# Rows chosen by a scatter through DRAM instead of a matmul, in a sigmoid-attention and mixture-of-depths kernel

## The chip, the cores and the metric

The kernel runs on one core of one Trainium2 chip. The metric is the device time of one execution in microseconds (us). Before the change three runs gave 446.25, 447.38 and 449.26 us; the median is 447.38.

## The reference, cut to what matters

Sigmoid attention for 8 sequences (12 heads, 448 tokens, head dimension 64), all in float32; its output, laid out as 8 x 448 x 768, goes into a mixture-of-depths block. There each token has a score (its row times `w_gate`), and in each sequence the 128 tokens of the highest scores go through a two-layer network and are added back, weighted by the sigmoid of the score.

```python
scores = scale * np.matmul(q, k.transpose(0, 1, 3, 2)) - np.log(S)
attn_out = np.matmul(1.0 / (1.0 + np.exp(-scores)), v)      # (8, 12, 448, 64)
x = attn_out.transpose(0, 2, 1, 3).reshape(8, 448, 768)
scores = np.einsum('bsd,d->bs', x, w_gate)
out = x.copy()
for b in range(8):
    top_idx = np.argpartition(-scores[b], 128)[:128]
    xe = x[b, top_idx]
    ye = np.maximum(xe @ w1, 0.0) @ w2                        # 768 -> 1024 -> 768
    g = 1.0 / (1.0 + np.exp(-scores[b, top_idx]))
    out[b, top_idx] = xe + g[:, None] * ye
```

## The kernel before, in words

**Steps and slots.** The 8 x 12 heads are 24 groups of four heads, three to a sequence. A step `s` (0 to 11) treats two groups, and has seven slots `n` (0 to 6), each for two of the fourteen 32-token pieces of each group. A slot issues 32 score matmuls (`score`, L339: k times q, into the two-bank PSUM tiles `PA[0]` and `PA[1]`), two sigmoids on ScalarE (`squash`, L353) and 32 value matmuls (`value`, L368, accumulating into the four PSUM banks `PO[x][pr]`, where `x` is the group of the step). The value matmuls run four slots behind the scores, so those of step `s - 1` end with slot 3 of step `s`. Then the accumulated outputs leave PSUM: `takes(s - 1, x)` are two transposes on VectorE (L389) for each `x`, into the sequence's rows `x_b`, which SyncE stores to `out` (L406).

**The order.** The schedule is manual: every engine, and every DMA queue, executes in the order in which the program issues; semaphores come from the tracked reads and writes of tiles. The function `after(s, n)` holds what follows slot `n`: loads, transposes of q and k on VectorE (L313, L321), gates, rankings, weight sums (`make_sum`, L208) and stores.

**Blocks.** In the steps named in `BLOCKS`, slot 3 is followed by a block of the mixture-of-depths network: `block(s)` (L680) runs the takes and a list of items. An item ("c", b) is the choice of sequence b's rows, ("t", b) turns the chosen rows (`turn_rows`, six transposes on TensorE at L524, copied by ScalarE), and (1, p, key) or (2, p, key) is one of the seven products of the first or the second layer of a pair of sequences p (a seven-product scheme with sums of weight quarters; L560 and L624, 12 or 4 matmuls in the program, each recorded twice). `places` gives each item its PSUM bank in turn. In steps whose successor has a block, and in the range `LATE` (from the first block's step on), the value matmuls are issued in another order (`first_slots`, `last_slot`, `rounds`, `split`): in `last_slot` the values of `x = 0` end before those of `x = 1`; in a `split` slot those of `x = 0` end last.

**From scores to rows.** When a sequence's rows are complete, `gate(b)` forms its scores on VectorE and GpSimd writes them to DRAM (L425); `spread(b)` reads them back into all 128 partitions (`rep`, L437, GpSimd's queue). `ranking(b)`, issued in the slot `RANKED[b]` (sequence 1: in step `FIRST`), counts for each token how many have a higher score or the same score and a lower number: eight passes over `rep` on VectorE (L445, L448). `place` adds the counts and compares them with the 128 places, a one-hot matrix (`hot`, L460). For sequences 2 to 5 VectorE multiplies the one-hot by row number and score and sums over four columns (L469, L473). `choose` (L482, L486) finishes with matmuls: row number and score by place, in PSUM. `fetch` copies them to SBUF (L493, L496) and gathers the rows from `out` with an indirect DMA on GpSimd's queue (L506); the result goes back to `out` with an indirect scatter on the same queue (L644). The last two sequences are treated in `rest`, after step 11.

**Values.** `load_v(s)` (L133) brings the values of a step: on SyncE's queue up to step 4, on ScalarE's from step 5 on.

## Time and profile before

| | us |
|---|---|
| runs, median (lowest to highest) | 447.38 (446.25 to 449.26) |
| profiled execution, its own time | 446.79 |
| its span | 445.0 |
| TensorE matmuls busy | 430.2 |
| VectorE busy | 302.6 |
| ScalarE busy | 191.2 |
| GpSimd busy | 32.8 |
| matmuls of the choices (L482, L486), all eight sequences | 6.4 |
| sums on VectorE for the choices (L469, L473) | 10.7 |
| one-hot on VectorE (L460), eight times | 5.5 |
| eight passes of all rankings (L445, L448) | 43.4 |

A line of the instruction views has start, duration, engine, source line, operation, output and inputs, their shapes, a count, and in brackets the idle time of the engine before it with what ended that. PE is TensorE's matmul, PEld its weight load, DVE VectorE, ACT ScalarE, POOL GpSimd, SP SyncE. A line of windows has the stretch, its length, the busy time of the five engines (with counts), the granted TensorE clock, the DMA engines' share and their GB/s.

### The profile page before, as it was taken

The page shows a single profiled execution, that of the slowest core. Times are in us where ns is not written, and L with a number is a line of the kernel's source. Part 1 is how long each engine was busy: PE and PEld are TensorE (multiplying, and loading weights), DVE is VectorE, ACT ScalarE, POOL GpSimd, SP SyncE. Part 2 cuts the span into 40 slices and gives each one's busy share as a digit, 9 for nine tenths or more (in the row PEclk, how much of TensorE's full clock was granted, in tenths as well). Part 3 has the DMA queues.
Part 4 walks back from the last instruction along what each step waited for, and adds up shares of the span by engine and source line. Part 5 has one row for each costly group of instructions (what it writes and reads, how often), then busy time and mean ns, then how long its engine had stood idle before and what let it go on. Part 6 is the DMA issues. An engine that isn't in the chain of part 4 may idle for free.

```text
span 445.0 us, 14349 instructions
## 1 busy us (share of the span) xinstructions
PE 430.2 (97%) x6374; PEld 259.2 (58%) x6374; DVE 302.6 (68%) x639; ACT 191.2 (43%) x257; POOL 32.8 (7%) x55
## 2 busy tenths in 40 slices
PE   7999999999999999999999999999999999999994
PEld 3456554444457568455447559546545749769952
DVE  4316368964958986966997885835796669883462
ACT  4666666666654633641660670552363330101100
POOL 7000000000001000100002000010000101001001
PEclk9999999999999999999999999999999999999998
DMA  8984835999645997699656598499945964611001
GB/s 234 246 249 110 300 87 114 212 186 232 200 143 120 233 308 186 181 234 298 219 181 177 154 234 147 138 224 241 269 167 107 190 219 63 119 36 72 1 0 71
DMA packets 112846, 76.80 MB, mean 173 GB/s; under 512 B 90304, under 2 KB 99136, under 8 KB 112784
## 3 DMA queue, kind: packets, MB, share of 16 engines
q1 hardware_dynamic: 106768, 61.55, 53.7%
q0 software_dynamic: 1984, 7.91, 6.2%
q10 hardware_dynamic: 4032, 6.42, 6.1%
q8 instruction: 50, 0.82, 0.8%
q14 instruction: 12, 0.10, 0.1%
HBM read 55.41 MB, written 20.46 MB: 170 GB/s over the span
## 4 chain that ended last, share of the span: by engine, by line
PE 88%; DVE 5%; ACT 3%; issue 1%; DMA 1%; POOLq 0%; ACTq 0%; DVEq 0%
PE a L339 27%; PE o L368 25%; PE o L624 12%; PE o L560 10%; PE a L560 7%; PE a L624 4%; ACT attn L353 2%; PE p L989 1%; DVE spare L208 1%; PE p L339 1%; DMA out_dram<-xe,idx 1%; ACT hidden L353 1%; DVE scr L448 1%; DVE scr L445 1%; DVE scr L397 1%
## 5 line engine op out<-in xcount | busy, mean ns | idle before, releaser
L339 PE MATMUL a<-qT,kT 32*64 32x448 f32 x2624 | 242.4, 537 | 0.6 <-DVE got L496 0.5
L353 ACT ACTIVATE attn<-a,bias_s 128x896 f32<-128x896 f32 x162 | 161.4, 1007 | 83.8 <-PE a L339 79.8
L368 PE MATMUL o<-attn,raw_v 32*64 32x448 f32 x2176 | 194.6, 536 | 0.5 <-issue 0.4
L339 PEld LDWEIGHTS a<-qT,kT 32*64 32x64 f32 x2624 | 92.8, 131 | 87.1 <-ACT attn L353 49.2
L368 PEld LDWEIGHTS o<-attn,raw_v 32*64 32x64 f32 x2176 | 74.3, 131 | 35.0 <-issue 26.9
L389 DVE STREAM_TRANSPOSE x_b<-o 128x448 f32<-128x448 f32 x48 | 27.8, 623 | 46.7 <-PE o L368 26.8
L368 PE MATMUL o<-attn,rows_t 32*64 32x448 f32 x448 | 42.3, 537 | 0.2 <-issue 0.2
L576 ACT ACTIVATE hidden<-hidden 128x512 f32<-128x512 f32 x12 | 7.5, 630 | 68.5 <-DVE hidden L573 68.5
L400 DVE TENSOR_REDUCE gate_p<-scr 128x14 f32<-128x448 f32 x48 | 29.8, 622 | 1.7
L321 DVE STREAM_TRANSPOSE kT<-raw_k 128x448 f32<-128x448 f32 x42 | 24.1, 613 | 8.8 <-DMA raw_k<-in_k_dram 7.6
L397 DVE TENSOR_TENSOR scr<-x_b,wg_b 128x448 f32<-128x448 f32 x48 | 29.4, 612 | 1.1
L573 DVE TENSOR_TENSOR hidden<-o,hidden 128x512 f32<-128x512 f32 x20 | 13.3, 688 | 21.1 <-PE o L560 20.9
L624 PE MATMUL o<-w_sb,hidden 128*128 128x384 f32 x80 | 27.4, 487 | 0.0
L635 DVE SCALAR_TENSOR_TENSOR xe<-o,gate,xe 128x384 f32<-128x384 f32 x36 | 20.5, 612 | 9.5 <-PE o L624 9.3
L313 DVE STREAM_TRANSPOSE qT<-qT 128x896 f32<-128x896 f32 x23 | 25.0, 1085 | 2.1 <-DMA qT<-in_q_dram 1.9
L448 DVE SCALAR_TENSOR_TENSOR scr<-rep,who,earlier 128x448 f32<-128x448 f32 (+1 forms) x32 | 21.8, 683 | 1.4
L560 PE MATMUL o<-rows_t,w_sb 128*128 128x128 f32 x192 | 22.7, 275 | 0.0
L560 PEld LDWEIGHTS o<-rows_t,w_sb 128*128 128x128 f32 x192 | 22.2, 192 | 0.3
L526 ACT ACTIVATE rows_t<-o 128x384 f32<-128x384 f32 x7 | 3.4, 484 | 43.9 <-PE o L524 43.9
L445 DVE TENSOR_SCALAR_CACHE_REDUCE scr<-rep,who 128x448 f32<-128x448 f32 (+1 forms) x32 | 21.5, 673 | 1.0
L368 PEld LDWEIGHTS o<-attn,rows_t 32*64 32x64 f32 x448 | 17.6, 131 | 6.4 <-issue 4.7
L624 PEld LDWEIGHTS o<-w_sb,hidden 128*128 128x128 f32 x80 | 14.7, 190 | 8.8
(114 smaller groups left out, 398.1 us busy)
## 6 DMA issues: line engine op xcount, KB each, us to landing
qT<-in_q_dram SPq DMA_DIRECT2D x24, 448.0 KB, 6.0
out_dram<-x_b SPq DMA_DIRECT2D x32, 336.0 KB, 8.8
raw_k<-in_k_dram SPq DMA_DIRECT2D x22, 448.0 KB, 5.1
spare<-sum SPq DMA_DIRECT2D x18, 384.0 KB, 5.7
raw_v<-in_v_dram ACTq DMA_DIRECT2D x28, 224.0 KB, 6.1
sum<-spare SPq DMA_DIRECT2D x8, 768.0 KB, 8.3
w_sb<-in_moe_w_dram SPq DMA_DIRECT2D x6, 768.0 KB, 7.1
rows_t<-in_v_dram SPq DMA_DIRECT2D x8, 224.0 KB, 5.1
```

Source lines behind the costliest of these rows:

```text
L313: nc.vector.transpose(heads["q", i], heads["q", i])
L321: nc.vector.transpose(kt[:, e], t[:, e].rearrange("p (a n) d -> p n a d", a=2))
L339: nc.tensor.matmul(out[y * Dh:(y + 1) * Dh, h % 2, :S], kt[d, e, r:r + 2].rearrange("d r t -> d (r t)"), qt[d, e], start=(e == 0), stop=(e ...
L353: nc.scalar.activation(a, psc[:, :, :S], AF.Sigmoid, bias=bias_s, scale=QK_SCALE)
L368: nc.tensor.matmul(PO[x][pr][j * Dh:(j + 1) * Dh, :S], raw_v[s][rows, 2 * pr + j, at:at + Dh], attn[s, pr, n][rows, j, :], start=((s, x, p ...
L389: nc.vector.transpose(x_tiles[b][:, :, 2 * g + pr, :], PO[x][pr][:, :S].rearrange("p (r t) -> p r t", t=TT))
L397: nc.vector.tensor_tensor(out=tmp, in0=x_tiles[b][:, :, hp, :], in1=wg_b[:, hp:hp + 1, :].to_broadcast([P, TB, TT]), op=ALU.mult)
L400: nc.vector.tensor_reduce(out=gate_parts[b][:, :, hp], in_=tmp, axis=AX.X, op=ALU.add)
L445: nc.vector.tensor_scalar(out=junk[:n], in0=rep[:n], scalar1=own, scalar2=0.0, op0=ALU.is_gt, op1=ALU.add, accum_out=above[:n, c:c + 1])
L448: nc.vector.scalar_tensor_tensor(out=junk[:n], in0=rep[:n], scalar=own, in1=earlier[:n, c, :], op0=ALU.is_equal, op1=ALU.mult, accum_out=l ...
L560: nc.tensor.matmul(ps[:, f, :n], w((t * FH + f) * P, P), x[:, t, :n], start=(t == 0), stop=(t == KH - 1))
L624: nc.tensor.matmul(ps[:n, :DH], h[:, t, :n], w(t * DH, DH), start=(t == 0), stop=(t == FH - 1))
```

## The change

For sequences 0 to 5 the choice no longer uses a one-hot or a matmul. A constant `listed` holds, for each token, its row number in the flattened `out` and a place for its score; `gate` writes the score beside the row number. `place` turns the counts into an integer `rank_of`, and four indirect DMAs on GpSimd's queue scatter the pairs (row number, score) into a DRAM table at the row of their rank; a plain load brings the first 128 rows back to SBUF as `chosen`, which holds the indices and the scores by place. The gather of the rows is issued in a slot of its own (`GATHERED`).

So there are no "c" items. Step 4 has no block, which makes it and step 3 plain steps and lets `LATE` begin with step 5. In a block all four takes are issued first, and `places` begins with `PO[0][0]` and `PO[0][1]` instead of `PA[1]`. The turns of the rows have other places: sequence 1's goes from block 5 to block 6, 2's and 4's from the end to the second place of their blocks. The rankings of sequences 3 and 5 move from slots (7, 6) and (10, 6) to (7, 2) and (10, 2). The values of step 5 are loaded on SyncE's queue, ahead of the block, and those of step 6 after the turn in block 6. The last two sequences are chosen as before.

```diff
--- before.py
+++ after.py
@@ -150,7 +150,7 @@
             y, odd = divmod(m, 2)
             rows = slice(m * TT, (m + 1) * TT)
             if s:
-                (nc.scalar if s > 4 else nc.sync).dma_start(
+                (nc.scalar if s > 5 else nc.sync).dma_start(
                     out=t[rows], in_=block(y, odd * NU, NU))
             else:
                 nc.sync.dma_start(out=t[rows, :, :NA * Dh], in_=block(y, odd * NA, NA))
@@ -260,13 +260,13 @@
 
     earlier = const.tile([P, NC, S], mybir.dt.uint8, name="earlier")
 
+    listed = const.tile([P, B - 2, NC, 2], I32, name="listed")
     who = [const.tile([P, NC, 2], F32, name=f"who{x}") for x in range(2)]
...
-    ones = const.tile([P, 1], F32, name="ones")
 
     def constants():
         make_identity(nc, iden)
@@ -281,7 +281,10 @@
 
         nc.gpsimd.memset(above, float(S))
         nc.gpsimd.memset(level, 0.0)
-        nc.gpsimd.memset(ones, 1.0)
+        nc.gpsimd.memset(listed, 0)
+        for a in range(4):
+            nc.gpsimd.iota(listed[a * TT:(a + 1) * TT, :, :, 0], pattern=[[S, B - 2], [1, NC]],
+                           base=a * NC, channel_multiplier=TB)
         for t in (gate_s, *who):
             nc.gpsimd.memset(t, 0.0)
         mine = moe.tile([P, NC], F32, name="place")
@@ -409,6 +412,12 @@
 
         return out[:b + 1].rearrange("b s d -> (b s) d")
 
+    def score_of(b):
+
+        if b < B - 2:
+            return listed[:, b, :, 1].bitcast(F32)
+        return who[b % 2][:, :, 1]
+
     def gate(b):
 
 
@@ -427,7 +436,7 @@
         nc.vector.transpose(by_token, total)
         for m in range(4):
             n = min(NC, TB - m * NC)
-            nc.vector.tensor_copy(who[b % 2][m * TT:(m + 1) * TT, :n, 1],
+            nc.vector.tensor_copy(score_of(b)[m * TT:(m + 1) * TT, :n],
                                   by_token[:, m * NC:m * NC + n])
         st[b]["scores"] = scores
 
@@ -440,7 +449,7 @@
     def rank(b, c):
         rep = st[b]["rep"]
         n = HELD[c]
-        own = who[b % 2][:n, c, 1:2]
+        own = score_of(b)[:n, c:c + 1]
         junk = moe.tile([P, S], F32, name="scr")
         nc.vector.tensor_scalar(out=junk[:n], in0=rep[:n], scalar1=own, scalar2=0.0,
                                 op0=ALU.is_gt, op1=ALU.add, accum_out=above[:n, c:c + 1])
@@ -449,60 +458,51 @@
             out=junk[:n], in0=rep[:n], scalar=own, in1=earlier[:n, c, :],
             op0=ALU.is_equal, op1=ALU.mult, accum_out=level[:n, c:c + 1])
 
-    def added(b):
-
-        return 1 < b < B - 2
-
     def place(b):
 
+        if b < B - 2:
+            rank_of = moe.tile([P, NC], I32, name="rank_of")
+            nc.vector.tensor_add(rank_of, above, level)
+            table = dram.tile([S, 2], I32, name="table")
+            for c, n in enumerate(HELD):
+                nc.gpsimd.indirect_dma_start(
+                    out=table, in_=listed[:n, b, c], in_offset=None,
+                    out_offset=bass.IndirectOffsetOnAxis(ap=rank_of[:n, c:c + 1], axis=0))
+            chosen = moe.tile([P, 2], I32, name="chosen", bufs=4)
+            nc.gpsimd.dma_start(out=chosen[:CAP], in_=table[:CAP])
+            st[b].update(idx=chosen[:, 0:1], picked=chosen[:, 1:2].bitcast(F32))
+            return
         nc.vector.tensor_add(place_s, above, level)
         st[b]["hot"] = moe.tile([P, NC, P], F32, name="hot")
         nc.vector.tensor_tensor(
             out=st[b]["hot"][:, :, :CAP], op=ALU.is_equal,
             in0=slots.rearrange("p (o i) -> p o i", o=1).to_broadcast([P, NC, CAP]),
             in1=place_s.rearrange("p (c o) -> p c o", o=1).to_broadcast([P, NC, CAP]))
-        if not added(b):
-            return
...
 
     def choose(b, ps):
 
-        if added(b):
-            for x in range(2):
-                nc.tensor.matmul(ps[:CAP, x:x + 1], st[b]["sums"][:, x, :CAP], ones,
-                                 start=True, stop=True)
-        else:
-            for c in range(NC):
-                nc.tensor.matmul(ps[:CAP, :2], st[b]["hot"][:, c, :CAP], who[b % 2][:, c, :],
-                                 start=(c == 0), stop=(c == NC - 1))
+        for c in range(NC):
+            nc.tensor.matmul(ps[:CAP, :2], st[b]["hot"][:, c, :CAP], who[b % 2][:, c, :],
+                             start=(c == 0), stop=(c == NC - 1))
         return b, ps
 
     def fetch(b, ps):
         n = CAP
-        idx = moe.tile([P, 1], I32, name="idx", bufs=5)
+        idx = moe.tile([P, 1], I32, name="idx", bufs=2)
         nc.vector.tensor_scalar(out=idx[:n], in0=ps[:n, 0:1], scalar1=float(b * S),
                                 scalar2=None, op0=ALU.add)
-        got = moe.tile([P, 1], F32, name="got", bufs=4)
+        got = moe.tile([P, 1], F32, name="got", bufs=2)
         nc.vector.tensor_copy(got[:n], ps[:n, 1:2])
+        st[b].update(idx=idx, picked=got)
+        gather(b)
+
+    def gather(b):
+        n = CAP
         if b == B - 1:
             xe = attn_tile(0, NU - 1).rearrange("p a s -> p (a s)")[:, :D]
         else:
             xe = moe.tile([P, D], F32, name="xe", bufs=3)
-        st[b].update(idx=idx, xe=xe, picked=got)
-        gather(b)
-
-    def gather(b):
-        n = CAP
+        st[b]["xe"] = xe
         nc.gpsimd.indirect_dma_start(
             out=st[b]["xe"][:n], out_offset=None, in_=rows_to(b),
             in_offset=bass.IndirectOffsetOnAxis(ap=st[b]["idx"][:n, 0:1], axis=0))
@@ -648,14 +648,13 @@
 
 
     BLOCKS = {
-        4: [("c", 0)],
-        5: [("c", 1), ("t", 0), (1, 0, 1), (1, 0, 2), ("t", 1)],
-        6: [(1, 0, 6), ("c", 2), (2, 0, 1), (1, 0, 7), (1, 0, 4), (1, 0, 5)],
-        7: [(1, 0, 3), (2, 0, 2), (2, 0, 5), (2, 0, 6), (2, 0, 3), ("t", 2)],
-        8: [("c", 3), (2, 0, 4), (2, 0, 7), (1, 1, 1), (1, 1, 2), ("t", 3)],
-        9: [("c", 4), (1, 1, 6), (2, 1, 1), (1, 1, 7), (1, 1, 4), (1, 1, 5)],
-        10: [(1, 1, 3), (2, 1, 2), (2, 1, 5), (2, 1, 6), (2, 1, 3), ("t", 4)],
-        11: [("c", 5), (2, 1, 4), (2, 1, 7), (1, 2, 1), (1, 2, 2), ("t", 5)],
+        5: [("t", 0), (1, 0, 1), (1, 0, 2)],
+        6: [("t", 1), (2, 0, 1), (1, 0, 6), (1, 0, 7), (1, 0, 4), (1, 0, 5)],
+        7: [(1, 0, 3), ("t", 2), (2, 0, 2), (2, 0, 5), (2, 0, 6), (2, 0, 3)],
+        8: [(2, 0, 4), (2, 0, 7), (1, 1, 1), (1, 1, 2), ("t", 3)],
+        9: [(1, 1, 6), (2, 1, 1), (1, 1, 7), (1, 1, 4), (1, 1, 5)],
+        10: [(1, 1, 3), ("t", 4), (2, 1, 2), (2, 1, 5), (2, 1, 6), (2, 1, 3)],
+        11: [(2, 1, 4), (2, 1, 7), (1, 2, 1), (1, 2, 2), ("t", 5)],
     }
 
     LENT = {(7, 4): [(1, 6, 2)], (8, 4): [(1, 7, 0), (1, 5, 1)],
@@ -679,25 +678,17 @@
 
     def block(s):
 
-        places = [PA[1][:, 0], PO[0][0], PO[0][1], PA[0][:, 0], PO[1][0], PO[1][1], PA[0][:, 0]]
-        work = BLOCKS.get(s, ())
-        if work and work[0][0] == "c":
-            chosen = choose(work[0][1], places.pop(0))
-        takes(s - 1, 0)
-        if work and work[0][0] == "c":
-            fetch(*chosen)
-            work = work[1:]
-        takes(s - 1, 1)
+        places = [PO[0][0], PO[0][1], PA[1][:, 0], PA[0][:, 0], PO[1][0], PO[1][1], PO[1][0]]
+        for x in range(2):
+            takes(s - 1, x)
         stores(s, NF)
         if s in FULL[::2]:
             gates(2 * s - 2)
-        for item in work:
+        for item in BLOCKS[s]:
             if item[0] == "t":
                 turn_rows(item[1], [places.pop(0) for _ in range(2)])
-                if item[1] == 0:
+                if s == 6:
                     load_v(s)
-            elif item[0] == "c":
-                fetch(*choose(item[1], places.pop(0)))
             else:
                 finish(item, begin(item, places.pop(0)))
 
@@ -916,7 +907,7 @@
 
         if n == NF and s:
             odd = s in FULL[1::2]
-            if s > 5:
+            if s == 5 or s > 6:
                 load_v(s)
             elif s < 4:
                 load_v(s + 1)
@@ -967,8 +958,11 @@
                 ranking(b)
         if n != NF:
             stores(s, n)
-
-    RANKED = [(3, 1), None, (6, 1), (7, 6), (9, 1), (10, 6), (11, 6)]
+        if (s, n) in GATHERED:
+            gather(GATHERED[s, n])
+
+    RANKED = [(3, 1), None, (6, 1), (7, 2), (9, 1), (10, 2), (11, 6)]
+    GATHERED = {(3, 3): 0, (4, 6): 1, (6, 2): 2, (7, 5): 3, (9, 2): 4, (10, 5): 5}
 
     first_outs = ExitStack()
 
```

## The prediction

> All times are microseconds of the profiled execution: 446.79 by its own time, with a span of 445.0, so 1.8 lie around the span. The runs shown have a median of 447.38 (446.25 to 449.26). The sum is made against 446.79; about 1% (4.5) is what a measurement of this kernel can tell from no change.
>
> **What bounds the kernel now.** First the page's busy times, then the instructions in order of time, engine by engine, around each block.
>
> ```profile
> PE 430.2 (97%) x6374; PEld 259.2 (58%) x6374; DVE 302.6 (68%) x639; ACT 191.2 (43%) x257; POOL 32.8 (7%) x55
> ```
>
> TensorE has 14.8 of idle time in all, and over half of it lies at the head (3.3) and behind the last matmul (6.1). So only two things are to be had: the TensorE work that goes, and the waits of 0.3 to 1.0 at the blocks. But whatever holds TensorE at a block is lost in full. VectorE, 68% busy on average, runs its instructions in program order, and is what can hold it. Its instructions ahead of blocks 7 and 10, its work between blocks 7 and 8, and TensorE at the head of blocks 7, 8 and 10:
>
> ```profile
> 190.94 1.72 DVE L208 TENSOR_TENSOR spare<-w_sb,spare 128x1536 f32<-128x1536 f32 x1
> 194.59 2.31 DVE L389 STREAM_TRANSPOSE x_b<-o 128x448 f32<-128x448 f32 x4 [1.93 <-ACT o L377]
> ...
> 227.28 0.16 DVE L458 TENSOR_TENSOR place_s<-above,level 128x4 f32<-128x4 f32 x1
> 227.48 0.69 DVE L460 TENSOR_TENSOR hot<-slots,place_s 128x512 f32<-128x512 f32 x1
> ...
> 292.76 1.17 DVE L321 STREAM_TRANSPOSE kT<-raw_k 128x448 f32<-128x448 f32 x2
> 301.55 1.18 DVE L389 STREAM_TRANSPOSE x_b<-o 128x448 f32<-128x448 f32 x2 [7.62 <-ACT o L377]
> ```
> ```profile
> 196.02 2.94 PE L560 MATMUL a<-rows_t,spare 128*128 128x128 f32 x24 [0.43 <-ACT attn L353]
> ...
> 232.69 1.56 PE L624 MATMUL o<-spare,hidden 128*128 128x384 f32 x4 [0.56 <-DVE x_b L389]
> ...
> 303.33 1.38 PE L560 MATMUL a<-rows_t,spare 128*128 128x128 f32 x10 [0.43 <-ACT attn L353]
> ```
>
> To be seen: before block 7 VectorE has a hole of 1.93 between its last job (done 192.66) and the takes of 194.59; before block 10 a hole of 7.62. Between blocks 7 and 8 it has none, and TensorE waits 0.56 for it at 232.69.
>
> **Gains.** Slot lengths are distances between the first score matmuls (L339) of slots. (1) Step 4. The c of block 4 occupies TensorE from 106.08 to 107.58: 1.5 go. The one-hot of sequence 0 (0.69 on VectorE) goes too, ahead of the takes of step 3; slot (3,4) is 3.5 long where (2,4) is 3.2: 0.4. Step 4's values now end in the early order: its last two slots took 3.8 and 3.1 for step 3 in that order, 3.8 and 2.9 for step 4 in the late one: −0.2. Together 1.7. (2) Block 5. It lasts from the last attention matmul's end (128.89) to 137.54, 8.65. After: the values of sequence part 0 end last here, so the first take is over 0.75 after that end and the second 1.35 after; ScalarE's copy (0.49) of the first three transposes ends at 1.75; then 24+24 matmuls at 2.7 per 24: 7.25. 1.4 go, and the two slots behind it, 3.36 and 3.53 long where the rest take 3.01, lose most of that excess because the turn of sequence 1, whose copies and differences stood there, is in block 6: 0.6. Together 2.0. (3) Block 6 gets that turn (0.75) and loses c (0.53) and the wait of 0.30; its differences (three of 0.56) end while (2,0,1) (2.6) runs. Nought; if they don't fit, up to 0.5 is lost. (4) Blocks 8, 9 and 11: the last attention matmuls end at 231.17, 266.27 and 338.48, and the first product starts at 232.69, 267.03 and 339.30. With c gone and bank PO[0][0] free as soon as the first take (0.6) is done, which ends before those times, 1.5, 0.75 and 0.8 go. Sum of gains 6.75. VectorE's one-hot and eight sums (0.69 and 2.8 for each of sequences 2 to 5) cost nothing in themselves: between blocks 7 and 8 the whole ranking leaves, which is part of the 1.5.
>
> **Losses.** The ranking of sequence 3 moves from slot (7,6) to (7,2), that of 5 from (10,6) to (10,2). Both now stand on VectorE ahead of the takes of the next block, and the block's first product waits for the first take, since it writes the bank that this take reads. One ranking takes 5.96 (221.49 to 227.45: eight passes of 0.68 with their read-outs, and the add at L458); with the first take and its signal 6.7.
>
> Block 7: VectorE is done at 192.66 with a chain that has run without a hole since block 6 ended. 192.66 + 6.7 = 199.35 for the first product, against 196.02: **3.3 lost**. Behind the ranking only the takes are queued, and TensorE waits for these.
>
> Block 10: a ranking needs its row of scores in all partitions (rep), and this comes late:
>
> ```profile
> 185.78 0.56 POOL L425 DMA_DIRECT2D scores<-total  x1 [8.59 <-DVE by_token L427]
> 187.78 0.57 POOL L437 DMA_DIRECT2D rep<-scores  x1 [1.43 <-DMA scores<-total]
> ...
> 292.04 0.57 POOL L425 DMA_DIRECT2D scores<-total  x1 [14.14 <-DVE by_token L427]
> 297.76 0.59 POOL L437 DMA_DIRECT2D rep<-scores  x1 [5.14 <-DMA scores<-total]
> ```
> ```profile
> DMA to landing us min/median/max: 7.1/7.1/7.1
> ```
>
> The second fence is the tile rep in the stretch from 297 on: landed at 297.76 + 7.1 = 304.8. (For sequence 3 the same question answers 3.8: 191.6, in time.) The hole of 7.62 is thus empty of data: VectorE would wait from 293.9 to 304.8, and the first product starts at 304.8 + 6.7 = 311.5 against 303.33: **8.2 lost**. Six lent weight halves and two stores stand before this row in the queues then; neither is changed.
>
> The clock: the last matmul ends at 438.93, and the granted clock of the last 3 us is
>
> ```profile
> 442.00:445.00 3.00, 0.00 (x0) 0.00 (x0) 0.00 (x0) 0.00 (x0) 0.00 (x0) 0.54 0.10 41
> ```
>
> With half speed for the rest that puts the fall near 442.25, 3.3 of idle after the last matmul. TensorE would idle 8.6 at block 10 and 3.8 at block 7. What the recovery costs no row of the middle shows: nothing (if the clock holds), up to another 3.3 at half speed, 1.65 lost, at each place. I take 1.7 for block 10 and half of it for block 7: 2.5, both ends kept. The Trainium skill ("TensorE: Matmul & The Clock Gate", "Why this matters for your kernels") wants no idle gap over about 3 us between bursts, or the clock falls back: it speaks against this change at both places. By its window of about 3.4 us at half clock, an estimate, the two would cost 3.4.
>
> **The new way to the rows.** Four scatters, a load, and the gather, all on GpSimd's queue. The table's scatters write one tile through indices, so each waits for the one before:
>
> ```profile
> 400.79 1.01 POOL L644 DMA_INDIRECT out_dram<-xe,idx  x1 [5.89 <-DVE xe L635]
> 404.68 0.98 POOL L644 DMA_INDIRECT out_dram<-xe,idx  x1 [2.88 <-DMA out_dram<-xe,idx]
> ```
>
> 3.9 from one to the next there; landings of that line range from 3.0 to 7.05, so 4 x 3.9 to 4 x 7, then a load of 1.6 to 5.4 (as scores) and 1 to issue the gather: 18 to 35 (6 if the scatters don't wait). Queued behind are the score rows. Sequence 2: ranked by 158.7, gather issued at 177 to 193; scores of 3 are due at 185.8. Sequence 4: 261.3, 280 to 296; scores of 5 due at 292.0. I take the quiet row, at which both are in time: cost nought. At the upper end the scores are 7 and 4 late, and blocks 7 and 10 that much more. The transposes come later: sequence 3's gather, after the scatter of output 0 at the end of block 7 (214) lands near 222 and is used near 240; 5's lands near 335 to 345 and is used near 355. Nothing is lost. The values of step 5 now come by SP, issued at the block's start: 4.6 to 6.1 to land, under the 7.25 of the block. GpSimd's five new set-up instructions (under 0.7 each) end long before 60.
>
> **Sum:** −6.75 + 3.3 + 8.2 + 2.5 = +7.2; 446.79 + 7.2 = **454.0**, 1.5% above the median.
>
> **Rivals.** A, the score row is early. If it lands for sequence 5 as it did for 3 (5.8 from the first issue instead of 12.8), at 297.85, block 10 starts at 304.55: 1.2 lost, no fall of the clock there. −6.75 + 3.3 + 1.2 + 0.4: 445.0, not slower. The total turns at a landing of 299.2 (a stall of 2.6). For it: 7.62 of hole, and only one of eight rows was so late; against: the congestion (the stretch 290 to 295 has the DMA engines busy throughout) has its cause in the program. B, the blocks are not held by the rankings at all, because the first product can go ahead of the takes: gains only, 440.0. Against it: TensorE waits 0.56 for the takes at 232.69 after a late ranking already. C, the scatters are slow, and hold back both score rows: 454.0 + 8 to 11, some 463. D, the change doesn't do what it says: were the scatters wholly in the shadow and rankings as good as before, B's number; I see no other form of it.
>
> **Chances.** The forecast (450 to 459) 0.62; A (443 to 449) 0.20; B 0.07; C 0.11. The range reaches from A's middle less 1, leaving out B and the lower half of A's spread, to the clear side of C: 444.0 to 461.0. Faster by over 1% (below 442.9): B and a little of A, 0.09. Within 1%: most of A and the forecast's lower edge, 0.21. Slower by over 1% (above 451.9): 0.70.
>
> **What would show it.** In the instructions in order of time: VectorE's L445 ahead of block 10 waiting for rep, and TensorE's first product of blocks 7 and 10 after an idle time of 3 to 4 and 8 to 9, released by the take (L389); no wait over 0.5 at blocks 8, 9 and 11; no L486 before 360; a granted clock under 1 near 200 and 312; scatters on GpSimd 4 apart. It goes wrong if the row for sequence 5 lands before 299, if VectorE reaches the ranking of 3 earlier, or if scatters hold the queue over 27.

## The result and the profile after

The changed kernel took 463.08 us (median of four runs, 461.20 to 470.42) against 446.94 before: a ratio of 1.0338, 95% interval 1.0278 to 1.0397. It is slower, as forecast (454.0), but the loss is more than twice the 7.2 of the sum, and the time lies 2 above the end of the range. A run that took over 1.5% more than the fastest of its kernel, here that of 470.42, counts in the medians but not in the ratios. The profiled execution took 463.73, its span is 461.8, 16.8 more than before.

First the page of the kernel after: the busy times, the granted clock in 40 slices, and by engine the chain of work that ended last.

```profile
PE 432.7 (94%) x6342; PEld 264.1 (57%) x6342; DVE 287.9 (62%) x589; ACT 191.4 (41%) x257; POOL 61.4 (13%) x89
...
PEclk9999999999999999989999999995999999999998
...
PE 57%; DMA 24%; DVE 8%; issue 6%; POOL 1%; ACT 1%; POOLq 0%; SPq 0%; DVEq 0%
```

TensorE has 32 matmuls fewer and is nevertheless busy 2.5 longer; it idles 14 more. A quarter of the chain is now DMA, against 1% before. Where TensorE waits, in the instructions of the kernel after in order of time (line numbers of the new kernel: L560 is a product, L524 a turn of rows, L392 a take):

```profile
162.44 1.08 PE L524 MATMUL o<-iden,xe 128*128 128x128 f32 x6 [2.83 <-DVE x_b L392]
...
202.37 3.88 PE L560 MATMUL o<-rows_t,spare 128*128 128x128 f32 x18 [3.89 <-DVE x_b L392]
...
316.43 1.86 PE L560 MATMUL o<-rows_t,spare 128*128 128x128 f32 x7 [8.52 <-DVE x_b L392]
```

Blocks 6, 7 and 10 start with a wait for the first take. Behind the third wait, on VectorE, stand the ranking of sequence 5 and the row that it waits for:

```profile
309.67 0.68 DVE L454 TENSOR_SCALAR_CACHE_REDUCE scr<-rep,listed 128x448 f32<-128x448 f32 x1 [10.12 <-DMA rep<-scores]
...
315.73 2.24 DVE L392 STREAM_TRANSPOSE x_b<-o 128x448 f32<-128x448 f32 x4
```

The first wait, at block 6, is the one that I did not foresee. VectorE waited there 4.97 for the score row of sequence 2 (landed at 155.8), and this is GpSimd's queue ahead of it:

```profile
122.49 1.13 POOL L468 DMA_INDIRECT table<-listed,rank_of  x1 [11.22 <-DVE rank_of L465]
126.44 0.98 POOL L468 DMA_INDIRECT table<-listed,rank_of  x1 [2.82 <-DMA table<-listed,rank_of]
131.98 0.92 POOL L468 DMA_INDIRECT table<-listed,rank_of  x1 [4.56 <-DMA table<-listed,rank_of]
137.47 0.91 POOL L468 DMA_INDIRECT table<-listed,rank_of  x1 [4.58 <-DMA table<-listed,rank_of]
139.80 0.58 POOL L472 DMA_DIRECT2D chosen<-table  x1 [1.42 <-DMA table<-listed,rank_of]
142.03 1.43 POOL L506 DMA_INDIRECT xe<-out_dram,chosen  x1 [1.65 <-DMA chosen<-table]
143.46 0.58 POOL L434 DMA_DIRECT2D scores<-total  x1
149.51 0.58 POOL L446 DMA_DIRECT2D rep<-scores  x1 [5.47 <-DMA scores<-total]
```

Each scatter waits for the landing of the one before (2.8 to 4.6). The scores of sequence 2 go out at 143.46, directly behind the gather; in the kernel before they went out at 136.34, when VectorE had them:

```profile
136.34 0.57 POOL L425 DMA_DIRECT2D scores<-total  x1 [4.46 <-DVE by_token L427]
```

How much this costs differs between executions. In the runs below whose program is the same up to there, these scores went out between 139.1 and 147.1; block 6 began without a wait in the two runs with 139.1 and waited up to 9.0 where they were later. The 2.7 in the table is the figure of this execution.

Where the 16.8 came from, by stretches between the same slots of both traces, with what the prediction had for each:

| stretch | predicted | measured |
|---|---|---|
| steps 0 to 2 | 0 | +0.6 |
| steps 3 to 5 with block 5 | −3.7 | −0.8 |
| block 6 | 0 | +2.7 |
| block 7 | +3.3 and clock 0.8 | +5.1 |
| block 8, block 9, block 11 | −1.5, −0.75, −0.8 | −1.6, −0.8, −0.9 |
| block 10 | +8.2 and clock 1.7 | +10.8 |
| slots between the blocks 6 to 11 | 0 | +0.2 |
| from slot (11,4) to the end | 0 | +1.5 |

The first row is a stall of 1.05 in slot (2,1), which in the trace of before stands in slot (10,2); it moves from execution to execution, and comes off again in the last but one row.

### The profile page after: what moved, and what is told of

The parts are those of the page before. It is cut to its first block, busy times and chain, and to the rows that moved or that the text cites. A ratio compares the mean times of both kernels' runs of the same rounds, so it can differ in the third digit from the quotient of the medians.

```text
span 461.8 us, 14273 instructions
## 1 busy us (share of the span) xinstructions
PE 432.7 (94%) x6342; PEld 264.1 (57%) x6342; DVE 287.9 (62%) x589; ACT 191.4 (41%) x257; POOL 61.4 (13%) x89
## 4 chain that ended last, share of the span: by engine, by line
PE 57%; DMA 24%; DVE 8%; issue 6%; POOL 1%; ACT 1%; POOLq 0%; SPq 0%; DVEq 0%
PE a L342 14%; PE o L371 14%; PE o L624 11%; DMA table<-listed,rank_of 10%; PE o L560 8%; PE a L560 6%; DMA rep<-scores 5%; PE a L624 3%; DMA scores<-total 3%; DVE scr L454 3%; DMA chosen<-table 3%; DVE scr L457 3%; DMA qT<-in_q_dram 1%; DMA raw_k<-in_k_dram 1%; DVE x_b L392 1%
## 5 line engine op out<-in xcount | busy, mean ns | idle before, releaser
L371 PE MATMUL o<-attn,raw_v 32*64 32x448 f32 x2176 | 196.7, 537 | 0.1
L371 PEld LDWEIGHTS o<-attn,raw_v 32*64 32x64 f32 x2176 | 77.1, 131 | 32.9 <-issue 25.5
L392 DVE STREAM_TRANSPOSE x_b<-o 128x448 f32<-128x448 f32 x48 | 27.7, 624 | 61.3 <-PE o L371 49.9
L468 POOL DMA_INDIRECT table<-listed,rank_of x24 | 23.5, 981 | 141.6 <-DVE rank_of L465 76.1
L560 PE MATMUL o<-rows_t,spare 128*128 128x128 f32 x216 | 30.0, 304 | 13.1 <-DVE x_b L392 13.1
L560 PEld LDWEIGHTS o<-rows_t,spare 128*128 128x128 f32 x216 | 28.8, 218 | 16.1 <-DVE x_b L392 16.1
L454 DVE TENSOR_SCALAR_CACHE_REDUCE scr<-rep,listed 128x448 f32<-128x448 f32 (+1 forms) x24 | 16.2, 674 | 17.7 <-DMA rep<-scores 17.1
L624 PE MATMUL o<-spare,hidden 128*128 128x384 f32 x72 | 24.3, 487 | 0.0
L560 PEld LDWEIGHTS a<-rows_t,w_sb 128*128 128x128 f32 x192 | 22.0, 192 | 0.8 <-ACT rows_t L526 0.3
L434 POOL DMA_DIRECT2D scores<-total x8 | 4.8, 601 | 132.8 <-DVE by_token L436 132.8
L560 PE MATMUL a<-rows_t,w_sb 128*128 128x128 f32 x192 | 22.4, 276 | 0.1
```

The source lines that it names most:

```text
L371: nc.tensor.matmul(PO[x][pr][j * Dh:(j + 1) * Dh, :S], raw_v[s][rows, 2 * pr + j, at:at + Dh], attn[s, pr, n][rows, j, :], start=((s, x, p ...
L392: nc.vector.transpose(x_tiles[b][:, :, 2 * g + pr, :], PO[x][pr][:, :S].rearrange("p (r t) -> p r t", t=TT))
L454: nc.vector.tensor_scalar(out=junk[:n], in0=rep[:n], scalar1=own, scalar2=0.0, op0=ALU.is_gt, op1=ALU.add, accum_out=above[:n, c:c + 1])
L468: nc.gpsimd.indirect_dma_start(out=table, in_=listed[:n, b, c], in_offset=None, out_offset=bass.IndirectOffsetOnAxis(ap=rank_of[:n, c:c + ...
L560: nc.tensor.matmul(ps[:, f, :n], w((t * FH + f) * P, P), x[:, t, :n], start=(t == 0), stop=(t == KH - 1))
L624: nc.tensor.matmul(ps[:n, :DH], h[:, t, :n], w(t * DH, DH), start=(t == 0), stop=(t == FH - 1))
```

## The experiments

**The rankings alone.** The kernel before, with nothing changed but two places:

```diff
-    RANKED = [(3, 1), None, (6, 1), (7, 6), (9, 1), (10, 6), (11, 6)]
+    RANKED = [(3, 1), None, (6, 1), (7, 2), (9, 1), (10, 2), (11, 6)]
```

> The kernel before, with only the rankings of sequences 3 and 5 moved to slots (7,2) and (10,2). Theory (a ranking ahead of the takes holds the block): block 7's first product still goes ahead of the takes in its PA[1] bank, its second one waits for the first take, some 0.5 us late; block 10's second product waits for a row of scores that lands near 305, then 6.7 of ranking and take: 5.4 late, and the clock falls there, 1.7 to 2.7; block 8 loses its wait of 1.1. 447 + 0.5 + 5.4 + 2 - 1 = 454 (452 to 457). Rival (the scatters and their queue are the cost, the rankings fit into VectorE's holes): 447, within 1.

Measured: 462.93 (462.24 to 464.30), ratio 1.0342 (1.0308 to 1.0376). In order of time, its two waits on TensorE (L624 is the second product of the block here, L389 the take):

```profile
204.14 1.01 PE L624 MATMUL o<-w_sb,hidden 128*128 128x384 f32 x1 [3.53 <-DVE x_b L389]
...
320.47 1.01 PE L624 MATMUL o<-w_sb,hidden 128*128 128x384 f32 x1 [9.07 <-DVE x_b L389]
```

Without one scatter, and with the first product in a bank that waits for no take, the place of two rankings costs 16. My expectation left out that in the kernel before the one-hot and eight sums (3.5 on VectorE) follow each ranking, so the takes come that much later: 0.5 + 3.5 and 5.4 + 3.5 are about the two waits. These 7 are not in the changed kernel, so that its loss is also 16 is a coincidence; what the run shows is that the place alone makes the waits.

**The bank of the first product.** The kernel after, with the old first place:

```diff
-        places = [PO[0][0], PO[0][1], PA[1][:, 0], PA[0][:, 0], ...]
+        places = [PA[1][:, 0], PO[0][0], PO[0][1], PA[0][:, 0], ...]
```

> The changed kernel, with PA[1] first again in the list of banks of a block, and nothing else. Theory (the low bank makes the first product wait for the takes): in blocks 7 and 10 the first product, 2.8 us, goes ahead of the takes, so each waits 2.8 less; block 7's wait drops to about 1 and its fall of the clock goes (1.7); blocks 8, 9 and 11 wait 0.3 to 0.4 more each for the sigmoid: 463.1 - 2.8 - 1.7 - 2.8 + 1 = 457 (455 to 459). Rival (VectorE's lateness is passed on whole, whatever the bank): 463.

Measured: 461.14 (456.19 to 464.52), ratio 1.0263 (1.0177 to 1.0350). In order of time, blocks 7 and 10:

```profile
199.61 2.94 PE L560 MATMUL a<-rows_t,spare 128*128 128x128 f32 x24 [0.34 <-ACT attn L356]
204.40 0.86 PE L524 MATMUL o<-iden,xe 128*128 128x128 f32 x4 [1.85 <-DVE x_b L392]
...
307.76 1.61 PE L560 MATMUL a<-rows_t,spare 128*128 128x128 f32 x13
315.76 0.48 PE L524 MATMUL o<-iden,xe 128*128 128x128 f32 x1 [6.38 <-DVE x_b L392]
```

The first product runs beside the ranking and hides 2 of each wait; block 7 is 2.9 shorter than in the kernel after, block 10 2.3. The range of its runs is too wide to tell that from the median alone, the trace tells it. The low banks are a part of the loss, not its cause.

**One ranking put back.** The kernel after with sequence 3 ranked in slot (7,6), its gather in (8,1) and its turn in block 9.

```diff
-    RANKED = [(3, 1), None, (6, 1), (7, 2), (9, 1), (10, 2), (11, 6)]
-    GATHERED = {..., (7, 5): 3, ...}
+    RANKED = [(3, 1), None, (6, 1), (7, 6), (9, 1), (10, 2), (11, 6)]
+    GATHERED = {..., (8, 1): 3, ...}
```

> The changed kernel, with the ranking of sequence 3 back at slot (7,6), its gather at (8,1) and its turn as the first item of block 9. Theory: block 7 loses its wait of 3.9 and its fall of the clock, 5.8 in all from the start of block 7 to the end of step 7; block 8 still starts without a wait over 0.5, since the one-hot and the sums are gone from VectorE; block 10 as in the changed kernel: 463.1 - 5.8 = 457.3 (456 to 459). Rival (the loss is contention from the scatters): 462 or more.

Measured: 457.72 (455.14 to 459.57), ratio 1.0219 (1.0165 to 1.0273). Block 7 starts with no wait and is 5.6 shorter, block 8 0.5; block 9 is 3.1 longer, since the turn of sequence 3 now stands there. Block 10, which nothing in this kernel touches, waits longer, by 2.9, which I did not expect and no run explains:

```profile
311.77 1.01 PE L560 MATMUL o<-rows_t,spare 128*128 128x128 f32 x3 [11.45 <-DVE x_b L392]
```

**The clock.** Useless matmuls on the identity, ahead of the first product of blocks 7 and 10, keep TensorE at work while it waits: first 6 and 14, then 16 and 36.

```diff
+        for _ in range({7: 16, 10: 36}.get(s, 0)):
+            nc.tensor.matmul(PA[1][:, 0, :P], iden, iden, start=True, stop=True)
```

> The changed kernel, with 6 matmuls of 128x128x128 without use ahead of the items of block 7, and 14 ahead of those of block 10, into PA[1], whose reader is done: they fill TensorE's waits (0.55 us each) and take nothing away. Theory (the clock's fall costs by itself): the records of half clock in the middle go, and with them half of the 3.4 at block 7 and of the 5.4 of matmuls at block 10: 463.1 - 1.7 - 2.7 = 458.7 (457.5 to 460). Rival (what the half clock delays is late anyway): 463.

> The changed kernel with 16 and 36 matmuls of 128x128x128 without use ahead of the items of blocks 7 and 10, into PA[1] (0.22 us each, 3.6 and 8.0 in all; 6 and 14 of them had filled only 1.6 and 3.4). Theory: no half clock in the middle; from the first product of each of the two blocks to the next score matmul 13.9 as in the kernel before, instead of 15.4 and 16.4: 463.1 - 1.5 - 2.5 = 459, give or take 3 for when the score rows land. Rival (the records' half clock costs nothing by itself): both blocks 15.4 and 16.4 long still.

Measured: 467.55 (461.88 to 471.16) and 463.96 (458.64 to 467.89; ratio 1.0313, 1.0269 to 1.0357). The first settles nothing: 6 and 14 of these matmuls filled only 1.6 and 3.4, and block 7 waited 9.3 in its profiled execution. There the scores of sequence 3 went out at 186.86, directly behind the gather of sequence 2: the chain of scatters held them as well. The second filled the waits. Windows around block 10 (busy times of PE, PEld, DVE, ACT, POOL, then the granted clock), first of the kernel after, then with the useless matmuls:

```profile
311.60:316.40 4.80, 0.00 (x0) 0.00 (x0) 4.47 (x15) 0.00 (x0) 0.50 (x1) 0.50 1.17 248
316.40:321.80 5.40, 5.37 (x25) 5.37 (x26) 1.57 (x3) 0.00 (x0) 1.73 (x3) 0.50 0.36 43
```
```profile
316.00:322.30 6.30, 5.56 (x51) 5.37 (x50) 5.91 (x19) 0.00 (x0) 0.54 (x1) 1.00 1.04 275
322.30:329.00 6.70, 6.70 (x41) 5.38 (x42) 5.19 (x9) 0.96 (x3) 2.29 (x3) 1.00 0.38 63
```

Without them the clock is at 0.50 for 5.4 of the block's own work, with them at 1.00. From the first product to the next score matmul the block takes 16.40 in the kernel after, 13.85 with the useless matmuls, and 13.85 before the change: the fall costs 2.55 here. At block 7 it is 15.46, 13.75 and 13.85: 1.6. The median did not fall to the 459 expected: in this profiled execution, near the top of its runs, block 6 waited 9.0 instead of 2.8.

**The chain of scatters.** If a scatter waits for the one before only since both write one table, four tables free them. The first attempt gives each sequence four tables and blanks all 24 with small stores at the start; the second has four tables for all sequences and four wide stores. GpSimd adds the four parts that it reads back.

```diff
-                    out=table, in_=listed[:n, b, c], in_offset=None,
+                    out=tables[c], in_=listed[:n, b, c], in_offset=None,
...
-            nc.gpsimd.dma_start(out=chosen[:CAP], in_=table[:CAP])
+            for c in range(NC):
+                nc.gpsimd.dma_start(out=parts[:CAP, c], in_=tables[c][b * S:b * S + CAP])
```

> The changed kernel, with four tables instead of one, blanked at the start: the four scatters of a sequence needn't wait for each other; the four parts are loaded and added on GpSimd. Theory (a chain of scatters holds GpSimd's queue for 20 us and the score row behind it): scatters 1 apart, the queue held some 9 to 10; the scores of sequence 2 go out when VectorE has them, the ranking of 2 begins near 151 and the wait of 2.8 at block 6 goes; blocks 7 and 10 as in the changed kernel. Some 42 more DMAs on GpSimd's queue may lengthen its closing drain by 0.06 each (2.4). 463.1 - 2.6 + 0 to 2.4: 460.5 to 463, block 6 without a wait over 0.5. Rival (the row for sequence 2 is late by the load on the DMA engines): block 6 still waits over 2.

> The changed kernel, with four DRAM tables (one for each scatter of a sequence, blanked by four wide DMAs at the start), so that the scatters needn't wait for each other; the four parts are loaded and added on GpSimd. Theory (the chain of scatters holds the queue and the score rows behind it): scatters some 1.3 apart, block 6 without a wait over 0.5, steps 3 to 5 up to 2 shorter; blocks 7 and 10 wait as in the changed kernel, 3.9 and 8.5; 22 more DMAs on GpSimd's queue lengthen the closing drain by 1 to 2. 463.1 - 2.7 - 2 + 1.5 = 460 (457 to 463). Rival (the scatters' own traffic is the load): no shorter.

Measured: 492.04 (486.31 to 497.29) and 460.72 (458.86 to 467.39; ratio 1.0327, 1.0283 to 1.0371). The first lost 27 at the head, where loads of q landed 16 us after issue in the median instead of 5.0; its middle agrees with the second. The first three scatters of the second, sequence 1, on GpSimd:

```profile
118.03 1.16 POOL L470 DMA_INDIRECT table<-listed,rank_of  x1 [15.25 <-DVE rank_of L467]
119.49 0.97 POOL L470 DMA_INDIRECT table<-listed,rank_of  x1 [0.30 <-issue]
120.77 0.91 POOL L470 DMA_INDIRECT table<-listed,rank_of  x1 [0.30 <-issue]
```

They are 1.3 to 1.5 apart instead of 4 to 5.5, the scores of sequence 2 go out at 135.53, and block 6 starts with no wait (3.2 less). Blocks 7 and 10 still wait 4.10 and 10.29.

**Both rankings put back**, with one table, with the 24, and with four. The edit is that of the kernel with one ranking put back, for sequence 5 too; with one table and with four, the values of step 9 are also loaded behind the turn in block 9.

> The changed kernel with one table as it is, but the rankings of sequences 3 and 5 back at (7,6) and (10,6), their gathers at (8,1) and (11,2), the turn of 3 first in block 9 with the values' load behind it. Theory: no wait over 1 at the heads of blocks 7 and 10, no half clock there, both blocks 13.9 long; the chain of 18 to 25 from the ranking of 5 to its landed rows ends after block 11's last product, where the turn of 5 waits 4 to 8. 463.1 - 5.8 - 11.3 + 0.5 + 6 = 452.5 (449 to 456). Rival (the route costs by contention): over 458.

> As with four tables, and the rankings of sequences 3 and 5 back at (7,6) and (10,6), gathers at (8,1) and (11,2), the turn of 3 first in block 9. Theory: the waits of blocks 6, 7 and 10 go, with the falls of the clock: 463.1 - 2.6 - 5.8 - 11.3 = 443.4, plus 2.4 for the drain, plus 0 to 2 for a late gather of 5 ahead of block 11's end: 445 (443 to 448). Rival (the scatter route costs by contention whatever the order): over 450.

> Both: four tables, and the rankings of sequences 3 and 5 back at (7,6) and (10,6). Theory: no wait over 1 at blocks 6, 7 and 10, no half clock in the middle, the rows of 5 land near the end of block 11's products, 0 to 1 of wait: 463.1 - 2.7 - 2 - 5.8 - 11.3 + 1.5 + 0.5 = 443.3 (441 to 446), faster than the kernel before. Rival (the scatter route costs whatever the order): 448 or more.

Measured: 460.59 (453.09 to 467.89), 478.21 (475.31 to 481.21; ratio 1.0741, 30 of it at the head) and 442.15 (441.58 to 442.59; ratio 0.9911, 0.9891 to 0.9932, 0.9% faster than the kernel before). In all three blocks 7 and 10 start with no wait: 5.6 and 11 less. With one table the chain holds the score rows of sequences 2 and 4 instead, as the profiled execution shows at blocks 6 and 9. It is the longest of the four; what the shortest, 453.09, waited for, no profile shows:

```profile
164.59 1.33 PE L524 MATMUL o<-iden,xe 128*128 128x128 f32 x5 [8.54 <-DVE x_b L392]
...
278.16 0.69 PE L524 MATMUL o<-iden,xe 128*128 128x128 f32 x2 [8.44 <-DVE x_b L392]
```

With four tables nothing over 0.9 is left in the middle. So far the two causes, rankings ahead of the takes and the chain, seemed to be the whole account.

**Is that version sound?** Two tables instead of four should have saved a little; 24 loads that nothing uses should have cost a little.

> Two DRAM tables of all six sequences instead of four (columns 0 and 2 into the first, 1 and 3 into the second), two part loads and two blank stores instead of four of each; late rankings as before the change. Issues on GpSimd's queue: 31 + 6 x 6 + 2 = 69, against 83 with four tables, 61 with one and 31 before. Theory (the length of the chain of scatters is what costs): the third and the fourth scatter wait once for a landing, 2 to 5.5, and two loads fewer wait behind them, so GpSimd holds the score rows some 12 to 17 us, as with four tables (16.5 from first scatter to gather), and no block waits for a score row: 442.15 less what the closing drain gives back. Theory of the drain (it grows with the number of issues on GpSimd's queue): from the start of the scores of slot (11,4) to the end it takes 94.36 with 31 issues, 95.88 with 61, 97.95 with 83, so some 96.4 with 69, 1.5 less: together 440.5 (439.5 to 442). Rival for the chain: any wait of a scatter for another is enough; then block 6 or block 9 waits 2 to 8 and the runs spread again: 444 to 452. Rival for the drain: it goes by the bytes or descriptors, or by what the last scatters carry, not by the number of issues: the tail stays at 97.9.

> Four tables with late rankings, and 24 small loads (128 rows of 8 bytes, into columns that nothing reads) added on GpSimd's queue in slots (2,0) and (2,4), far from the end and from any score row: 107 issues instead of 83. Theory (the closing drain grows with the number of issues): the tail from slot (11,4) to the end is 0.06 to 0.1 for each of the 24 longer, 99.4 to 100.3 instead of 97.95, and the time 443.6 to 444.5 where nothing else is held. Rival (the drain waits for work that is still under way at the end, or for the scatters into the tables): the tail stays at 97.95 and the time at 442. Second thing looked at: whether small loads delay wide loads away from the head as 24 small stores did at the head (some 27 us there): then slots of steps 2 and 3 wait for q, k or v by more than 2.

Measured, on another chip: 455.97 (454.12 to 458.39; ratio 1.0204, 1.0171 to 1.0238) and 470.59 (two runs; ratio 1.0536, 1.0488 to 1.0583). No block waits over 1.4 in either, but slots in which scatters are under way grew: (3,4), (5,1), (5,2) and (11,2) took 4.7, 5.0, 5.4 and 6.6 with two tables, 6.9, 4.9, 6.8 and 9.1 with the loads, where the kernel with four tables took 3.2, 3.0, 3.8 and 3.8. Four runs on one chip were to tell whether this belongs to the kernels or to the chip:

> The kernel with four tables and late rankings once more, unchanged, beside the one with two tables on one chip. Theory S (scatters hold TensorE, by an amount that is the chip's or the job's, not the kernel's): where two tables take 454 to 456, this one takes 452 to 458 too, with slots (3,4), (5,1), (5,2) and (11,2) at 4.5 to 7 instead of 3.0 to 3.8. Theory T (it comes with two tables or with more loads): 442 again, these slots 3.0 to 3.8, whatever two tables take.

> The kernel with two tables and late rankings once more, unchanged. Theory S: as the four tables on this chip but for the drain (1.4 less) and for the waits of the third scatter: both at 441 to 442 or both at 452 to 458. Theory T: 455 again.

> The kernel before with, behind each ranking of sequences 0 to 5, a sum of 0.16 on VectorE and four scatters of row number and score into four DRAM tables that nothing reads: the one-hot way still finds the rows. It measures the scatters alone: 24 issues more on GpSimd's queue. Drain: tail 94.36 + 24 x 0.06 to 0.08 = 95.8 to 96.3. Theory S, on a chip that shows it: six places with 1.5 to 3.5 lost each at the slots behind the rankings, so 446.8 + 1.6 + 9 to 18 = 457 to 466; on a chip that doesn't: 448 to 449. Theory T: 448 to 449 anyway.

> The changed kernel once more, unchanged, on the chip of the three others. Theory S, on a chip with the holds: 463 + 5 to 10; on one without: steps 3 to 5 gain 2.6 to 3.5 on the kernel before instead of 0.8, and the time is 459 to 463, by what block 6 waits (0 to 9). Theory T: 463, steps 3 to 5 as they were.

Measured: 468.62 (466.95 to 469.82; ratio 1.0475), 455.61 (454.70 to 456.43; 1.0177), 466.52 (463.61 to 470.77; 1.0404, 1.0339 to 1.0470) and 462.85 (461.29 to 466.86; 1.0365). The very kernel that took 442.15 on one chip takes 468.62 on this one, more than either theory had, while the kernel before takes 446.2 and 446.4 on the two. And 24 scatters that nothing reads, added to the kernel before, cost 18 to 20:

```diff
+            for c, n in enumerate(HELD):
+                nc.gpsimd.indirect_dma_start(
+                    out=tables[c], in_=who[b % 2][:n, c], in_offset=None,
+                    out_offset=bass.IndirectOffsetOnAxis(ap=rank_of[:n, c:c + 1], axis=0))
```

Windows behind the first four scatters (issued 82.72 to 87.71), first with them, in the longest of the four executions (470.77), then in the kernel before:

```profile
86.00:88.00 2.00, 1.98 (x14) 0.70 (x14) 2.00 (x4) 0.00 (x0) 1.41 (x2) 1.00 0.99 131
88.00:90.00 2.00, 1.57 (x18) 0.67 (x17) 1.93 (x4) 1.01 (x1) 0.00 (x0) 0.72 0.95 163
90.00:92.00 2.00, 2.00 (x32) 1.41 (x29) 1.90 (x4) 0.00 (x0) 0.00 (x0) 0.50 0.88 198
```
```profile
86.00:88.00 2.00, 2.00 (x46) 0.76 (x44) 2.00 (x3) 1.37 (x2) 0.00 (x0) 1.00 0.92 127
88.00:90.00 2.00, 2.00 (x56) 0.91 (x55) 1.89 (x4) 1.16 (x2) 0.00 (x0) 1.00 0.88 214
```

The count of matmuls (x14, x18 against x46, x56) is what to read. The busy time hides it: 14 matmuls of 0.53 to 0.59 each, spread over 2.00, still cover it. TensorE's issue falls to a third while VectorE runs on undisturbed; in this execution the clock then falls to 0.50 as well. Busy DMA engines are not needed for that. In the kernel with four tables and late rankings on this chip, during the scatters of sequence 5 (issued 346.20 to 350.86), the count falls as far with the DMA engines all but idle (share 0.01 and 0.02):

```profile
348.00:350.00 2.00, 2.00 (x14) 0.40 (x7) 0.00 (x0) 0.94 (x1) 1.39 (x3) 1.00 0.01 1
350.00:352.00 2.00, 1.40 (x9) 0.55 (x9) 0.00 (x0) 0.06 (x1) 2.00 (x3) 1.00 0.02 1
```

The last pair asked whether the indices do it:

> The kernel before with 24 scatters that nothing reads, once more, unchanged. If the hold of TensorE goes with every chip: 463 to 470, slots (3,4), (5,1), (5,2) and (11,2) at 4.5 to 9 as in its first run. If it is the chip's: 448 to 449 where the chip is free of it, these slots 3.0 to 3.8.

> The kernel before with 24 plain stores of 128 rows of 8 bytes in the places of the 24 scatters, same queue, same number of issues and the same bytes, no indices. Theory I (the indirection does it): 448 to 449, that is the drain alone (1.4 to 1.9) with no slot held, while the scatters beside it cost 17 to 24. Theory P (any small store from this queue does it): as the kernel with the scatters on the same chip. If the scatters cost nothing on this chip either, this run tells nothing.

Measured, on the chip of the four: 468.08 (465.25 to 474.61; ratio 1.0446) with scatters, 458.72 (457.63 to 459.74; 1.0259, 1.0208 to 1.0311) with plain stores of the same bytes. The scatters hold TensorE behind five of the six rankings (slot (11,2) 9.0 against 3.8). The plain stores leave (5,1), (5,2), (9,2) and (11,2) as they were, but lengthen (3,6), block 5, (6,4) and block 8 by 1.4, 3.7, 2.1 and 4.2; in block 8, 3.21 of this is a wait for the gathered rows, not a hold. Both theories hold in part. These two ran on the same chip as the four before. That the hold goes with the chip, and not with the hour, thus rests on two chips free of it and two that show it: all kernels with scatters that ran with the 442.15 are free, and so are the two with 24 tables, which ran on a chip of their own and have (3,4), (5,1), (5,2) and (11,2) at 3.2, 3.0, 3.8 and 3.8. Only the kernel with four tables and late rankings is known to have run on a chip of each sort. What it is that keeps TensorE's instructions back, no view here shows.

## Why the prediction was right or wrong

**Losses.** The two places and the mechanism were right. TensorE idles 3.46 more at block 7 and 8.09 more at block 10 than the 0.43 it idled there before; the steps said 3.3 and 8.2. The kernel with the rankings alone and the kernels with late rankings show it: with the place the waits come and go, whatever finds the rows. Rival A (the row lands early) fell: the row of sequence 5 landed at 309.6, 1.7 after block 10 could have begun (307.9), for 1.5 in the steps and 5.5 ahead in A. Rival B (the blocks are not held) fell. The step that the first product waits for the take, since it writes its bank, holds too: with the old bank 2 of each wait go.

**The clock** was mis-sized: 2.5 in the sum, 1.6 + 2.55 = 4.15 measured, above the upper bound that I gave for block 10 (1.65). I bounded the recovery by the 3.3 of idle that bring the fall; the clock stays at 0.50 for 10.2 from 311.57 on, of which 5.4 are the block's own work. At block 7 it is 3.4, all of it the block's work. The Trainium skill ("TensorE: Matmul & The Clock Gate", "Why this matters for your kernels") says that a gap of over some 3 us lets the clock fall back; both gaps here, 3.89 and 8.52, did so. The estimate of 3.4 from its window was nearer than mine, and short as well.

**The queue.** "I take the quiet row, at which both are in time: cost nought" is the step that failed. The time was right: 19.5 from sequence 1's first scatter to its gather, 24.6 for sequence 2 and 21.4 for sequence 4, in the 18 to 35 given. But I checked only whom sequences 2 and 4 hold up (the scores of 3 and 5, blocks 7 and 10). Sequence 1's scatters stand ahead of the scores of sequence 2, and block 6 waits for these: +2.7. The four tables take that wait away. Rival C named 463 for slow scatters, and the time hit its number by luck, not by its mechanism: in this execution GpSimd stood idle 0.87 and 7.24 ahead of the scores of 3 and 5. For 3 that was close; with one ranking put back, and with the few useless matmuls, its scores went out directly behind the gather of 2, as rival C had it.

**Gains.** Blocks 8, 9 and 11 gave 1.6, 0.8 and 0.9 for 1.5, 0.75 and 0.8. Steps 3 to 5 gave 0.8 for 3.7. The kernels that have the same program up to there gave 0.9 (old bank) to 1.5 (few useless matmuls) on one chip, and the changed kernel itself 1.0 there; on another chip 2.6 (many useless matmuls) and 3.5 (both rankings late). The sum of the edits is thus worth about what the steps say where nothing holds TensorE, but the terms are not: the slot of block 5 is only 0.4 shorter, for 1.4, since the block lasts 7.5 (the steps said 7.25, where their own terms add up to 7.15) and the matmuls ahead of it in the slot take 0.7 longer; (5,4) and (5,5) give 0.8 for 0.6, and (4,2), which the sum did not have, gives 0.9. The scatters take it back, slot by slot, where they hold TensorE, which the sum put at nothing without a reason: (3,5), (4,0) and (5,2) are 0.5 to 0.9 longer than before. That scatters can do that, the kernel before with 24 scatters shows; that they do all of the 2.9 here is argued from the slots, not shown.

**The end.** The sum had no term for it; it is 1.5, and every kernel here with more DMAs on GpSimd's queue has it.

So the sign and the larger half of the loss were read off the profile; the miss (9 of time) is 2.9 of gains held back by the scatters, 2.7 at block 6, 1.6 of the clock and 1.5 at the end.

## What to carry to other kernels

When an operation moves to a queue, go through everything behind it in that queue and price each, the nearest one first; I checked the rows of 3 and 5 and not that of 2. A data-dependent job on an in-order engine goes behind the transfers that free the next stage, not ahead of them, however empty the hole looks: the hole was there since its data were not. A detour of small rows through DRAM is to be measured by itself, on more than one chip, before a schedule is built around it: the best schedule here was 0.9% faster on one chip and 4.8% slower on another.

## What the runs showed of the hardware

**A closing time that grows with GpSimd's DMAs.** After the last scatter the kernel ends 4.2 later before the change, 5.9 after it:

```profile
439.87 0.97 POOL L644 DMA_INDIRECT out_dram<-attn,idx  x1 [4.19 <-DVE attn L635]
```
```profile
455.02 0.96 POOL L644 DMA_INDIRECT out_dram<-attn,idx  x1 [4.20 <-DVE attn L635]
```

The spans end at 445.0 and 461.8. From slot (11,4) to the end it is 94.36 with 31 DMAs on that queue, 95.88 with 61, 96.53 with 69, 97.95 with 83, 99.65 with 107. The 24 loads that nothing uses, issued 400 us earlier, add 1.70: 0.05 to 0.1 for each DMA, whenever it was issued.

**Small rows from GpSimd's queue hold TensorE's issue**, on some chips: four scatters of 128 rows of 8 bytes, unchained, cost up to 5.5 at a slot, those chained in one table up to 0.9, and on two chips none of it was seen. It comes with the DMA engines at a share of 0.01 too. The cause is open.

**A clock that falls through thin work.** The granted clock fell to 0.50 not only after idle gaps, but also, in one execution, behind a stretch in which TensorE issued 14 matmuls in 2 us instead of 46. In the changed kernel the stretches at half speed last 3.41 (202.34 to 205.75) and 10.24 (311.57 to 321.81). Those of the other runs, leaving out the one that the end of each run cuts short, last 3.41, 6.83, 10.24, 13.65 or 17.07: whole multiples of 3.41. So a fall is priced in such steps, by when it begins and when the matmuls are back, and not by the idle time alone.
